# Scores by first and last 64 tokens instead of by even and odd tokens, in a fused gated-recurrence and bilinear FFN kernel

## The chip, the cores and the metric

The kernel runs on one core of one Trainium2 chip. The metric is the device time of one execution in microseconds (us); the number given for a kernel is the median of its runs. About 0.3% (0.6 us here) is what a measurement of this kernel can tell from no change.

## What is computed

A gated linear recurrence over 768 tokens, for 4 batches of 8 heads with head size 48, followed by a bilinear feed-forward network (FFN) over all 3072 tokens:

```
for t in range(S):                                   # S = 768, D = 48
    state = alpha[:, :, t, :, None] * state + einsum('bhd,bhe->bhde', k[:, :, t], v[:, :, t])
    y[:, :, t] = einsum('bhd,bhde->bhe', q[:, :, t], state)
x = y.transpose(0, 2, 1, 3).reshape(B * S, H * D)    # 3072 x 384
out = ((x @ w_a) * (x @ w_b)) @ w_out                # w_a, w_b 384 x 1536, w_out 1536 x 384
```

## The kernel before, in words

**Chunks.** The recurrence is computed in chunks. A chunk holds 256 tokens of two batches, and there are six (0 to 5). Each batch of a chunk is a "u" (0 or 1). A partition holds two neighbouring tokens, called r = 0 and r = 1 (even and odd); 128 partitions hold 256 tokens. The upper and the lower 64 partitions are two groups g of 128 tokens each. Within a group the attention is done directly, with a triangular mask; between groups a 48x48 state per head is carried.

**Order of the work.** `PROGRAM` is a list written out in full: each entry is a chunk number and operations, and the instructions of every engine are issued in exactly that order. There is no scheduler on the chip: a waiting instruction holds up all that stands behind it on its engine. The last letter of an operation names its engine: V VectorE (DVE in the profile), S ScalarE (ACT), P GpSimd (POOL), Y the queue of SyncE (SP).

**One chunk, operation by operation** (line numbers of the profile of before):

- `ld` (L549) loads alpha, k, q, v; `W` and `Wo` load the FFN's weights on GpSimd's queue.
- `ln`, `l2`/`l2s` (L564, L613), `H`/`L` or `R` (L623), `A2` or `AQ` (L633), `ra`, `E` (L667): logarithms of alpha, their sums of two tokens, the running sum on TensorE, the exponentials. `l2s` works on 64 partitions and moves them to the other 64.
- `lv` (L652) scales k and q of the r = 0 tokens, `mk` and `mq` (L678) write the scaled keys and queries into `QKp`.
- `C` + `Ce` (L736, L742, L744; chunks 0 and 1) or `T` (L767; chunks 2 to 5, a DMA transpose on SyncE's queue) transpose `QKp` into `kqT`.
- `v` (L785, L787) copies v from the loaded tile `v_t` into `vx`, whose heads stand 96 columns apart with zeros between.
- `K`/`K2` (L799, L812) and `k` (L826 to L830) update the state; `dk`, `de` or `dr`, `dl` supply its decay.
- `D` (L841) computes scores, `M` (L846) masks them on the way out of PSUM, or `Mc` (L850) copies them out and `Mm` (L854) masks the copy.
- `SB`, `SA` and `Y` (all through L865) sum y from the carried state and from the masked scores; `X` (L900, L902) copies y out of PSUM into `xT`.
- `a`, `b` (L919), `as` (L925), `pr` (L933), `o` (L941), `ot` (L956, L958), `st` (L974): the FFN. `a` and `b` each are 3 matmuls for one 128-wide block of the hidden layer; a `*` stands for all 512 tokens of the chunk, 0 or 1 for one half. `pr` multiplies the two, `o` is half of the output sum of 128 tokens (6 matmuls).

The FFN of chunk c is interleaved with the preparation of chunk c+1.

**Scores and inner sums before.** The keys of one parity rk (64 of them in a group) are the stationary operand, all 128 queries of the group the moving one, so that each matmul is 64x64 times 64x128. The four matmuls of the two groups g and of the two heads r of a pair sit in the four quadrants of the TensorE array and run side by side; four such matmuls are called a quad below. `D` is 4 quads, `Y` is 12. Tokens in y, `xT` and the scaled keys stand ordered by parity, and `pr` puts them back in order when it writes `prod`:

```
        o_, a_, b_ = tokens(ch.prod[:, f, :], us), columns(a[:, :n], n), columns(b, n)
        nc.vector.tensor_mul(o_, a_, b_)
```

Of the kernel before, what the change touches and what calls it, by code (L numbers as in the profile page):

```python
# [9 lines left out]
BF16 = mybir.dt.bfloat16  # L10
# [7 lines left out]
0: cm 0; c1; cz 0 b P; ci; ld a 0b Y; c1a; ld a 0a Y; ln 0b; cu; cz 1 b P; fill 7 2; cu2 V; cz 0 q V; cus; ld k 0b Y; ld k 0a Y; B 0b 5; ld q 0b Y; ld v 0 P  # L18
0: ln 0a; ld q 0a Y; E 0b b; E 0b i; mq 0b V; B 0a 0; E 0a i; dk 0 2; E 0a b; ld a 1 P; mk 0b V; C 0 1 5; cs 0 m P; ld k 1 P; ld q 1 P; v 0 S; mk 0a V; cm 1
0: de 0; fill 2 1; mq 0a V; C 0 0 3; Ce 0 1 V; W b 0 256; cz 0 v P; Ce 0 0 V; D 0 1 4; ln 1; ld v 1 P; W a 256 768; K 0 0 6; k 0 0 V; M 0 1; D 0 0 0; SB 0 6  # L20
0: cz 1 q P; B 1a 2; M 0 0; W a 0 256; E 1a i; E 1a b; W b 256 768; mq 1a V; mk 1a V; B 1b 4; dk 1 3; E 1b i; E 1b b; de 1; v 1 S; mq 1b V; mk 1b V; C 1 0 0
0: Y 0; SA 0; Ce 1 0 V; cs 1 m P
1: ld a 0 P; ld a 1 P
0: W a 768 1536; C 1 1 1; X 0 S; c2 P; D 1 0 3; W b 768 1536
1: ld q 0 P
0: Ce 1 1 V; K 1 0 5; k 1 0 V; a 4 0 0
1: ld k 0 P
0: D 1 1 6; SB 1 1
1: ld v 0 P; ld q 1 P
0: Mc 1 0; a 3 0 5; Wo 0 6; a 0 0 3; Mm 1 0 V; Mc 1 1; as 0 0; b 0 0 4  # L30
1: ld k 1 P
0: pr 0 0; b 1 0 6; a 2 0 3; a 1 0 7; a 5 0 4; as 2 0; b 2 0 3; Mm 1 1 V; as 1 0; b 4 0 7; as 5 0; b 5 0 4; pr 2 0; pr 1 0
1: ln 0
0: SA 1; Y 1; Wo 6 12; K 1 1 6; as 3 0; as 4 0; X 1 S
1: ra 0
0: K 0 1 3
1: l2 0 V
0: b 3 0 0; pr 5 0; pr 4 0
1: H 0 V; L 0 V
0: a 2 1 1; a 5 1 2; as 5 1; pr 3 0; a 1 1 7; b 4 1 5; b 5 1 4; as 2 1; k 0 1 V; pr 5 1; a 4 1 2; as 1 1  # L40
1: ln 1
0: b 2 1 0; pr 2 1; a 6 * 3; as 4 1; b 1 1 2
1: l2 1 V
0: pr 4 1; as 6 *
1: H 1 V
0: pr 1 1
1: A2 0 7
0: a 11 * 0; a 7 * 5; a 0 1 4
1: L 1 V
0: k 1 1 V  # L50
1: ra 1
0: as 11 *
1: lv 0 q V; E 0 i
0: as 0 1; b 6 * 0; b 11 * 3; a 8 * 4; pr 6 *; pr 11 *
2: ld a * P
0: b 0 1 1; as 8 *; a 3 1 6
1: E 0 b; lv 0 k V
0: a 10 * 2; pr 0 1
1: mq 0 V; ld v 1 P
0: b 8 * 4  # L60
1: A2 1 7
0: as 10 *; b 10 * 2; pr 8 *
1: E 1 b
0: as 3 1; as 7 *; b 9 * 3; b 3 1 0; b 7 * 1; a 9 * 6
2: ld q * P
1: v 0 S; lv 1 q V; mk 0 V
0: pr 10 *
1: mq 1 V; C 0 1 4
0: as 9 *
1: C 0 0 2  # L70
0: o 0 0 5; pr 7 *
1: dk * 6
2: ld k * P
3: ld v * P
0: cz 1 v P; pr 9 *
1: Ce 0 0 S; E 1 i; de *; lv 1 k P; Ce 0 1 V; D 0 1 1; D 0 0 3
0: pr 3 1
1: Mc 0 0; K2 0 0 7 0
0: o 1 0 6
1: mk 1 V; M 0 1  # L80
0: o 3 0 4; o 1 1 -; ot 1 S; c3 P
3: ld a * P
0: cs 1 0 P; o 3 1 -
1: k 0 0 V; k 0 1 V; Mm 0 0 V; SB 0 1; C 1 0 3; C 1 1 7
0: ot 3 S; o 0 1 -
1: Ce 1 0 V
2: ln *
1: v 1 V; D 1 0 3; Ce 1 1 S; K2 1 1 6 0; Y 0; SA 0
0: ot 0 V
1: k 1 0 V; D 1 1 6  # L90
0: o 2 0 5
1: M 1 0
2: l2 0 V
1: X 0 S; a 3 0 1; Mc 1 1
2: l2s 0 P; l2s 1 P
1: a 2 0 3; a 4 0 4
2: R 0
1: k 1 1 V; as 4 0
2: ra 1
1: as 3 0; b 4 0 7  # L100
0: o 2 1 -
1: as 2 0
0: ot 2 S
1: pr 4 0
2: R 1; lv 1 q P
1: b 3 0 6; b 2 0 7; a 5 0 2; pr 3 0; b 5 0 3; as 5 0; b 1 0 5; a 1 0 1; pr 5 0; pr 2 0; a 7 0 2; as 1 0; pr 1 0
2: AQ 3
1: SB 1 6
2: lv 0 k P
1: a 10 0 5  # L110
2: lv 1 k V; ra 0; ld v * P
1: Mm 1 1 V
2: E 1 b
1: as 10 0; b 10 0 0; pr 10 0
2: mq 1 V; E 1 i
1: as 7 0; b 7 0 1
2: E 0 b; E 0 i
1: a 0 0 5
0: st 3 Y
2: dr  # L120
1: SA 1; Y 1
2: mk 1 V
1: pr 7 0; a 11 0 0; a 6 0 3; b 6 0 2; X 1 S; b 11 0 4; a 2 1 6; as 6 0; a 3 1 7; as 11 0; b 2 1 1; pr 6 0
2: lv 0 q V
1: b 4 1 0; as 2 1
2: T 1
1: pr 11 0
2: dl
0: st 0 Y
1: a 0 1 2; pr 2 1  # L130
2: mq 0 V
1: b 3 1 3; b 0 0 6; as 3 1; as 0 0; b 0 1 7; pr 3 1; a 8 0 1; a 9 0 5
0: st 1 Y
1: b 8 0 3; b 9 0 4; pr 0 0; as 0 1
2: mk 0 V
1: a 4 1 2
3: ln *
1: a 9 1 6; pr 0 1; as 8 0; b 9 1 1
3: ra 1
1: b 10 1 7; pr 8 0; a 10 1 3; as 4 1; as 9 0; as 9 1; a 6 1 6; b 6 1 2; b 11 1 5; pr 4 1; as 10 1; pr 9 0; a 11 1 4; pr 10 1; pr 9 1; as 6 1  # L140
2: v 1 S
1: a 8 1 3; b 8 1 1; a 7 1 6; pr 6 1
3: l2 0 V
1: as 11 1
2: T 0
1: as 8 1; a 5 1 4
3: ra 0
1: as 5 1; a 1 1 2
2: v 0 V
4: ld a * Y  # L150
1: pr 11 1; as 7 1; pr 8 1
2: K2 * * 0 7; D 1 1 3; D 1 0 5
1: as 1 1; b 5 1 2; o 2 0 1
2: k * 0 V
1: pr 5 1
3: v 0 S; v 1 S
1: b 1 1 2
2: Mc 1 0; M 1 1
3: l2s 0 P; l2s 1 P
1: b 7 1 0; o 2 1 -; pr 1 1; o 3 0 4  # L160
2: SB 0 5
# [12 lines left out]
2: Mc 0 1
4: ln *
3: ld q * Y; ld k * Y
2: k * 1 V
3: AQ 2
2: Y 1; SA 1; Mm 0 1 V; Mm 0 0 V; Y 0; X 0 S
3: E 0 b  # L180
4: l2 0 V
2: X 1 V
1: o 0 1 -
2: b 1 * 6; a 1 * 5
3: E 1 b
4: ld k * Y
3: E 1 i
1: ot 0 S
3: E 0 i
4: l2s 0 P  # L190
2: a 0 * 0; b 0 * 1; as 0 *; as 1 *
3: lv 0 k P; lv 0 q P
2: a 5 * 7
1: st 3 Y
2: a 7 * 4
4: l2s 1 P
2: a 2 * 5
3: lv 1 q V; mq 1 V; lv 1 k V
2: pr 1 *
3: dr  # L200
2: pr 0 *
3: mk 0 V
4: ld q * Y
0: st 2 Y
2: as 5 *; a 6 * 6; b 6 * 2; as 7 *
3: mq 0 V
2: b 9 * 4; b 7 * 0
1: st 2 Y
3: dl
4: R 0  # L210
2: b 5 * 7
1: o 1 0 3
2: a 9 * 1; pr 7 *; as 6 *
3: T 0
2: pr 6 *
4: ra 0
2: pr 5 *; a 11 * 6
3: mk 1 V
2: as 9 *; a 3 * 0
4: lv 0 k V; lv 0 q V; R 1  # L220
2: as 2 *
1: o 1 1 -
2: as 11 *; a 8 * 5; b 11 * 2; a 4 * 7; b 2 * 1
3: T 1
1: ot 1 V
2: pr 9 *; as 8 *; pr 11 *; pr 2 *; b 8 * 3; b 4 * 5; as 4 *
5: ld a * Y
3: K2 * * 4 6
2: pr 8 *; as 3 *; pr 4 *
3: k * 0 V; D 0 0 2; Mc 0 0  # L230
2: b 3 * 1
4: ra 1
2: pr 3 *; b 10 * 5; a 10 * 0
# [171 lines left out]
def kernel(  # L405
# [14 lines left out]
    C = 128  # L420
# [678 lines left out]
```

## Time and profile before

| | |
|---|---|
| median of 3 runs | 193.84 us (193.75 to 194.29) |
| span of the profiled execution | 192.0 us (the page gives no other time of it) |
| TensorE busy | 186.8 us, 97% of the span |
| VectorE busy | 133.1 us, 69% |
| ScalarE busy | 106.5 us, 55% |
| GpSimd busy | 56.9 us, 30% |
| granted TensorE clock | 1.00 |

The median lies 1.8 us above the profiled span; what lies around the span is start and end of the execution. An engine's busy time is the union of its instructions. Matmuls are pipelined: one takes about 0.2 us from start to end while the next starts some ns later, so the pace of matmuls is read from how far a group of them reaches, not from the duration of one.

### The profile page before, as it was taken

Reading aid. Unit: us, or ns where it says so; the run is one execution under the profiler, and the core shown is the slowest. Engines: PE = TensorE matmul, PEld = TensorE weight load, DVE = VectorE, ACT = ScalarE, POOL = GpSimd, SP = SyncE. Lnnn points to the kernel's source line nnn. Section 1 sums busy time; section 2 is a strip of 40 time slices with the busy share of each in tenths; the row PEclk is TensorE's granted clock in tenths of the full one; section 3 lists DMA queues with packets and bytes.
Section 4 is the critical chain, followed back from the end, with each engine's and each line's share of the span. In section 5 each row is a group of like instructions: output and inputs, shape, how many; then the busy total and the mean of one; then the engine's idle time right before and its main releaser. Section 6 shows DMA issues by size and latency. Waiting matters only on the chain.

```text
span 192.0 us, 6086 instructions
## 1 busy us (share of the span) xinstructions
PE 186.8 (97%) x2613; PEld 116.9 (61%) x2613; DVE 133.1 (69%) x223; ACT 106.5 (55%) x194; POOL 56.9 (30%) x75
## 2 busy tenths in 40 slices
PE   7999999999999999999999999999999999999992
PEld 3888875677778876645557444656465644545562
DVE  2387698994989888899897956887567446252510
ACT  4448885656779867753487756743572435314211
POOL 8999626752450500640074262000000000000000
PEclk9999999999999999999999999999999999999999
DMA  5999999999969999999999989017641200000422
GB/s 132 274 219 218 251 253 235 244 269 264 251 107 166 165 216 265 248 254 149 233 213 181 156 174 129 3 42 140 146 66 44 85 0 0 0 0 3 164 82 82
DMA packets 62618, 29.40 MB, mean 153 GB/s; under 512 B 53712, under 2 KB 60768, under 8 KB 62592
## 3 DMA queue, kind: packets, MB, share of 16 engines
q0 software_dynamic: 18432, 13.37, 39.6%
q1 hardware_dynamic: 44016, 15.55, 38.1%
q8 instruction: 20, 0.33, 0.7%
q10 hardware_dynamic: 144, 0.10, 0.2%
q14 instruction: 6, 0.05, 0.1%
HBM read 25.98 MB, written 4.74 MB: 160 GB/s over the span
## 4 chain that ended last, share of the span: by engine, by line
PE 91%; DMA 5%; SPq 1%; DVE 1%; issue 1%; ACT 0%; DVEq 0%
PE psum L919 47%; PE psum L941 24%; PE psum L865 7%; PE psum L841 3%; DMA kqT<-QKp 3%; DMA q_t<-in_q_dram 3%; PE psum L736 2%; PE psum L633 1%; PE psum L952 1%; SPq L549 1%; PE psum L799 1%; PE psum L812 1%; PE psum L700 1%; PE psum L591 1%; PE psum L592 1%
## 5 line engine op out<-in xcount | busy, mean ns | idle before, releaser
L919 PE MATMUL psum<-xT,wb_t 128*128 128x512 bf16 (+1 forms) x270 | 56.0, 337 | 0.0
L919 PE MATMUL psum<-xT,wa_t 128*128 128x512 bf16 (+1 forms) x270 | 56.0, 337 | 0.0
L941 PE MATMUL psum<-wo_t,prod 128*128 128x384 bf16 x276 | 49.4, 326 | 0.0
L919 PEld LDWEIGHTS <-wb_t 128*128 128x128 bf16 x270 | 25.9, 98 | 19.9 <-issue 0.5
L919 PEld LDWEIGHTS <-wa_t 128*128 128x128 bf16 x270 | 25.9, 98 | 19.7 <-issue 0.3
L941 PEld LDWEIGHTS <-prod 128*128 128x128 bf16 x276 | 25.9, 98 | 17.6
L956 ACT ACTIVATE ot<-psum 128x384 f32<-128x384 f32 (+1 forms) x16 | 7.7, 482 | 22.7 <-PE psum L941 21.6
L850 ACT ACTIVATE m<-psum 128x1024 bf16<-128x1024 f32 x14 | 14.1, 1023 | 4.6 <-PE psum L841 4.3
L613 POOL TENSOR_TENSOR l<-la 64x384 f32<-64x384 f32 x7 | 7.8, 1108 | 26.6 <-ACT la L556 19.0
L846 DVE TENSOR_TENSOR m<-psum,mask 128x1024 bf16<-128x1024 f32 x10 | 12.1, 1220 | 3.1 <-PE psum L841 3.1
L652 POOL TENSOR_TENSOR q_t<-q_t,ra 128x384 f32<-128x384 f32 x5 | 6.1, 1215 | 22.5 <-ACT ra L645 19.7
L556 ACT ACTIVATE la<-a_t 128x1536 f32<-128x1536 f32 (+2 forms) x9 | 9.5, 1055 | 2.3 <-DMA a_t<-in_alpha_dram 2.2
L678 DVE TENSOR_TENSOR QKp<-q_t,beta 128x768 bf16<-128x768 f32 x10 | 10.0, 995 | 1.0 <-ACT beta L667 1.0
L865 PE MATMUL psum<-m,vx 64*64 64x128 bf16 x576 | 10.5, 217 | 0.0
L900 ACT ACTIVATE xT<-psum 128x768 bf16<-128x768 f32 x9 | 7.2, 816 | 5.7 <-PE psum L865 5.5
L678 DVE TENSOR_TENSOR QKp<-k_t,invb 128x768 bf16<-128x768 f32 x10 | 9.7, 972 | 0.8 <-ACT invb L667 0.8
L854 DVE TENSOR_TENSOR m<-m,mask 128x1024 bf16<-128x1024 bf16 x14 | 9.3, 684 | 1.2 <-ACT m L850 1.2
L958 DVE COPY ot<-psum 128x384 f32<-128x384 f32 (+1 forms) x9 | 4.8, 532 | 7.6 <-PE psum L941 4.7
L865 PEld LDWEIGHTS <-vx 64*64 64x64 bf16 x576 | 9.0, 107 | 0.5 <-issue 0.3
L841 PE MATMUL psum<-kqT 64*64 64x128 bf16 x384 | 9.0, 219 | 0.4 <-DMA kqT<-QKp 0.3
L652 POOL TENSOR_TENSOR k_t<-k_t,a_t 128x384 f32<-128x384 f32 x6 | 7.4, 1228 | 6.1 <-issue 3.3
L549 POOL DMA_DIRECT2D v_t<-in_v_dram x8 | 8.5, 1058 | 0.1
(271 smaller groups left out, 287.9 us busy)
## 6 DMA issues: line engine op xcount, KB each, us to landing
out_dram<-ot SPq DMA_DIRECT2D x23, 192.0 KB, 3.8
q_t<-in_q_dram SPq DMA_DIRECT2D x3, 768.0 KB, 6.5
a_t<-in_alpha_dram POOLq DMA_DIRECT2D x2, 768.0 KB, 15.2
k_t<-in_k_dram POOLq DMA_DIRECT2D x2, 768.0 KB, 12.1
v_t<-in_v_dram POOLq DMA_DIRECT2D x4, 384.0 KB, 7.0
a_t<-in_alpha_dram SPq DMA_DIRECT2D x2, 768.0 KB
k_t<-in_k_dram SPq DMA_DIRECT2D x2, 768.0 KB
a_t<-in_alpha_dram POOLq DMA_DIRECT2D x3, 384.0 KB, 8.5
```

The source lines that it names most:

```text
L549: eng.dma_start(out=t[:, us, hs].rearrange("p b h r d -> p (b h) (r d)"), in_=src[ch.b0 + us.start:ch.b0 + us.stop, hs, ch.s * 2 * C:(ch.s ...
L556: nc.scalar.activation(out=ch.la[:, us, hs].rearrange("p b h r d -> p (b h r d)"), in_=ch.a[:, us, hs].rearrange("p b h r d -> p (b h r d) ...
L613: eng.tensor_add(ch.l2[(1 - g) * HC:(2 - g) * HC, 1], x[:, :, 0, :], x[:, :, 1, :])
L652: eng.tensor_mul(x, x, by)
L678: eng.tensor_mul(QKp[ch.c % 2][:, u, j, :, hs, :D], src[:, u, hs].rearrange("p h r d -> p r h d"), f)
L841: nc.tensor.matmul(s2[g * HC:(g + 1) * HC, r, p, rk, :], lhsT=turned_part(ch, u, 1, rk, 2 * h + p, g, rs), rhs=queriesT(ch, u, 2 * h + p, ...
L846: nc.vector.tensor_mul(m.rearrange("p r a k s -> p (r a) (k s)"), ch.s2[u, h].rearrange("p r a k s -> p (r a) (k s)"), maskn(4))
L850: nc.scalar.activation(out=m.rearrange("p r a k s -> p (r a) (k s)"), in_=ch.s2[u, h].rearrange("p r a k s -> p (r a) (k s)"), func=AF.Copy)
L854: eng.tensor_mul(x, x, maskn(4))
L865: nc.tensor.matmul(y[c * DP:(c + 1) * DP, g, j // 2 * C:(j // 2 + 1) * C], lhsT=lhsT, rhs=rhs, start=(g, c) not in begun, stop=False, skip ...
L919: nc.tensor.matmul(p, lhsT=(wa_t, wb_t)[w][:, kk, f * 128:(f + 1) * 128], rhs=ch.xT[:, kk, us, :], start=(kk == 0), stop=(kk == KT - 1))
L941: nc.tensor.matmul(op, lhsT=ch.prod[:, f, at:at + C], rhs=wo_t[:, f, :], start=(f == 0), stop=(f == NFF - 1))
```

## The change

1. **Scores and inner sums.** Keys are taken by halves of a group: x = 0 is its first 64 tokens, x = 1 its last 64. Keys of x = 1 are seen only by queries of the last 64 tokens, so half of the matmuls in `D` and in `Y` have a moving operand of 64 columns instead of 128 (192 of 384 and 288 of 576). The number of instructions on TensorE stays the same.
2. **Masks.** Scores, mask and masked scores have 192 columns for a head pair and r instead of 256: `M`, `Mc` and `Mm` work on 128x768 instead of 128x1024.
3. **Keys.** The transposed keys must stand by halves. After `C` the transposes themselves write them so; after `T` a new operation `Tr` copies 128x1024 from `kqT` into a new tile `kp` (8 copies: 5 on VectorE, 3 on ScalarE).
4. **Values.** `v` still copies all of v; a new operation `vs` then copies, for one u and one g, two pieces of 32 partitions x 384 into the other 32 partitions (48 copies: 20 VectorE, 22 ScalarE, 6 GpSimd). `K` and `K2` now read v from `v_t`, not from `vx`.
5. **y.** `X` is done for each g apart (24 of 128x384: 11 VectorE, 13 ScalarE, where there were 12 of 128x768) and writes the tokens in order; `xT` is laid out by batch first. `pr` has no reordering any more.
6. **Placing.** The list is written anew. `l2s` is all on VectorE (8; before 1 there, 7 on GpSimd), `lv` is 16 on VectorE and 4 on GpSimd (before 9 and 11), `v` is 8 on VectorE and 4 on ScalarE (before 3 and 9). The loads of GpSimd's queue keep their order up to the last weights; the load of chunk 5's keys goes to SyncE's queue.

The core of the diff:

```diff
-            ch.kqT[u] = wk.tile([C, 2, 2, P2, C], BF16, name="kqT", bufs=4)
+            ch.kqT[u] = wk.tile([C, 16 * C], BF16, name="kqT", bufs=4)
...
+    def turn_keys(ch, u, eng):
+        t = alloc_t(ch, u)
+        x = wk.tile([C, 8 * C], BF16, name="kp", bufs=3)
+        ch.kp[u] = x.rearrange("p (h a q w) -> p h a q w", h=2, a=2, q=4)
+        ch.qT[u] = t[:, :8 * C].rearrange("p (r h a s) -> p h a r s", h=2, a=2, r=2)
+        evict(x.rearrange("p (y r s) -> p y r s", r=2, s=HQ), t[:, 8 * C:].rearrange("p (r y s) -> p y r s", r=2, s=HQ), eng)
...
+    def vswap(ch, us, g, eng):
+        for x in range(2):
+            to, of = (slice(g * HC + n * HQ, g * HC + (n + 1) * HQ) for n in (x, 1 - x))
+            o_ = vxs[ch.c % 2][to, us, 1 - x, :, :D]
+            i_ = ch.v[of, us, :, x, :]
...
+            evict(o_, i_, eng)
...
-            for rk in range(2):
+            for x in range(2):
                 for g in range(2):
                     for r in range(2):
                         rs = slice(r * DP, (r + 1) * DP)
-                        nc.tensor.matmul(s2[g * HC:(g + 1) * HC, r, p, rk, :], lhsT=turned_part(ch, u, 1, rk, 2 * h + p, g, rs),
-                                         rhs=queriesT(ch, u, 2 * h + p, g, rs), start=True, stop=True)
+                        nc.tensor.matmul(s2[g * HC:(g + 1) * HC, r, p, cols(x)], lhsT=keysT(ch, u, 2 * h + p, g, rs, x),
+                                         rhs=queriesT(ch, u, 2 * h + p, g, rs, x), start=True, stop=True)
...
-                        out_mm(ch, u, g, h, j, vx[gs, u, rk, at:at + DP], ch.m[u, h // 4][gs, h % 2, h // 2 % 2, rk, :])
+                        m = ch.m[u, h // 4][gs, h % 2 * 2 + h // 2 % 2, cols(x)].rearrange("p (r s) -> p r s", r=2)
+                        out_mm(ch, u, g, h, j, vx[gs, u, x, at:at + DP], m, x)
...
-            ch.xT = wk.tile([128, KT, B, C], BF16, name="xT")
...
+            ch.xT = wk.tile([128, B, KT, C], BF16, name="xT")
+        evict(ch.xT[:, 2 * u + g].rearrange("p a (s r) -> p a r s", r=2),
+              ch.y[u][0][:, g, :KT * C].rearrange("p (a r s) -> p a r s", a=KT, r=2), eng)
...
-        o_, a_, b_ = tokens(ch.prod[:, f, :], us), columns(a[:, :n], n), columns(b, n)
-        nc.vector.tensor_mul(o_, a_, b_)
+        nc.vector.tensor_mul(ch.prod[:, f, us.start * C:us.stop * C], a[:, :n], b)
```

The list, for the start of chunk 0 and for chunk 3's preparation beside chunk 2's FFN:

```diff
-0: ln 0a; ld q 0a Y; E 0b b; E 0b i; mq 0b V; B 0a 0; E 0a i; dk 0 2; E 0a b; ld a 1 P; mk 0b V; C 0 1 5; ...
+0: ld q 0b Y; B 0a 0; dk 0 4; E 0b i; mk 0b V; ld v 0 P; E 0b b; mq 0b V; C 0 1 5; ...
...
+2: Y 0; X 1 0 V
...
+1: o 1 0 0; o 1 1 -
...
+2: X 0 1 S; X 0 0 S; X 1 1 V; a 3 * 7; a 4 * 2; b 0 * 3; b 3 * 4; a 5 * 5; as 3 *; a 0 * 7
...
+3: T 0
+2: pr 9 *
+3: T 1
...
+5: ld q * Y; ld k * Y
...
+3: Tr 0 V
```

798 lines of the change are left out of this document (371 added, 427 removed).

## The prediction

> **What bounds the kernel now.** I read the page's busy times first, then its chain of work that ended last, then the windows by stage, then TensorE's timeline for the pace of the small matmuls, then the groups by form for what VectorE has to take over.
>
> ```profile
> span 192.0 us, 6086 instructions
> PE 186.8 (97%) x2613; PEld 116.9 (61%) x2613; DVE 133.1 (69%) x223; ACT 106.5 (55%) x194; POOL 56.9 (30%) x75
> PE 91%; DMA 5%; SPq 1%; DVE 1%; issue 1%; ACT 0%; DVEq 0%
> ```
>
> TensorE is busy for 97% of the span and is 91% of the chain. The windows cut at TensorE's own marks: the first FFN matmul (18.30) and the end of the last `Y` of chunks 1, 2, 3 and 4 (57.47, 78.06, 105.27, 130.88).
>
> ```profile
> core 0: us, PE busy (x) PEld busy (x) DVE busy (x) ACT busy (x) POOL busy (x), PEclk, DMA share, GB/s
> 57.47:78.06 20.59, 20.59 (x414) 16.22 (x415) 18.38 (x37) 15.59 (x29) 3.50 (x4) 1.00 1.18 204
> 78.06:105.27 27.21, 27.21 (x399) 14.71 (x400) 24.04 (x34) 16.89 (x29) 10.22 (x9) 1.00 1.07 212
> 105.27:130.88 25.61, 25.32 (x356) 13.43 (x356) 20.24 (x28) 15.15 (x27) 5.54 (x5) 1.00 0.65 98
> 57.47:130.88 73.41, 73.12 (x1166) 44.35 (x1167) 62.65 (x97) 47.62 (x84) 19.25 (x17) 1.00 0.95 170
> 18.30:188.69 170.39, 170.06 (x2342) 103.91 (x2336) 122.67 (x201) 96.33 (x175) 39.82 (x39) 1.00 0.76 148
> ```
>
> From 18.3 to the last matmul TensorE idles 0.3 us of 170, at full clock. So a column less on TensorE there is time, if nobody else becomes late; and the one that could is VectorE, at 62.65 of 73.41 us (85%) in the three middle stages, not at the 69% of the average.
>
> **TensorE's part.** Half of the quads of `D` and `Y` go from 128 to 64 columns. What a quad costs is its pace, read from how far a run of them reaches:
>
> ```profile
> 67.86 0.63 PE L841 MATMUL psum<-kqT 64*64 64x128 bf16 x32
> 94.61 0.69 PE L812 MATMUL psum<-vx,QKp 64*64 64x48 bf16 x64
> 129.01 0.87 PE L865 MATMUL psum<-m,vx 64*64 64x128 bf16 x48
> ```
>
> One matmul lasts 0.22 us (0.19 at 48 columns). So 32 with 128 columns step by (0.63 - 0.22)/31 = 13.2 ns, 48 by (0.87 - 0.22)/47 = 13.8 ns: 54 ns a quad. The 48-column ones of the state step by (0.69 - 0.19)/63 = 7.9 ns: 32 ns a quad. No row has 64 columns. In proportion to columns it would be 27 ns, the 48-column row says not below 32; I take 33, near that row because its weights have the same 64x64 form. That saves 21 ns a quad. Halved quads are 12 x 2 x 2 = 48 of `D` and 12 x 6 = 72 of `Y`; the 10 of chunk 0's first u lie before 18.3, where TensorE waits for others. 110 x 21 ns = **2.3 us**, between 0 and 110 x 27 ns = 3.0. Strided moving operands (two runs for queries) are in the 54 ns already, so `xT` by batch costs nothing; strided writes to PSUM (half of the `Y` matmuls, 32 transposes) no row shows: I take nothing for them, as for the strided reads, and if they ran at the pace of 128 columns the saving would go to the end 0.
>
> The Trainium skill, "TensorE: Matmul & The Clock Gate", sections "LDWEIGHTS (loading the stationary operand)" and "The mechanism", speaks against this: a weight load takes its columns divided by 1.2 in ns, and overlaps running matmuls only in another row group; for 64 columns that is an estimated 53 ns, and halving columns would bring nothing. The 48-column row, with the same weights at 32 ns a quad, does not agree. It is the second rival below.
>
> **The start.** The chain begins with the load of q.
>
> ```profile
> 7.81 0.56 DVE L678 TENSOR_TENSOR QKp<-q_t,prod 128x384 bf16<-128x384 f32 x1 [3.63 <-DMA q_t<-in_q_dram]
> 8.29 1.06 DVE L678 TENSOR_TENSOR QKp<-k_t,prod 128x384 bf16<-128x384 f32 x2
> 8.94 0.62 PE L736 MATMUL psum<-ident,QKp 128*128 128x128 bf16 x8 [0.15 <-DVE QKp L678]
> ```
>
> Before, `mq 0b` waits for q and `mk 0b` comes behind it, although k is loaded ahead of q. Now `mk 0b` comes first, so the transposes can start after `mq 0b`, at about 8.4 instead of 8.94. Further on, `B 1b` no longer stands behind `M`'s waits, `K` needs no copied v, and y is evicted by two engines (0.55 each beside the other, instead of 0.82). Following the new list with these rows, the first FFN matmul comes at about 18.6 with everything of chunk 0's second u ahead of it issued, which before is reached at about 19.2. I take **-0.5 us**, from 0 to -1.0: the first weights land near 18.5 (issue at 12.08, 6.4 us to landing) in the unchanged order of GpSimd's queue.
>
> **VectorE's part.** Rows used, with those that the change replaces:
>
> ```profile
> L846 DVE TENSOR_TENSOR m<-psum,mask 128x1024 bf16<-128x1024 f32 x10 | 12.1, 1220 | 3.1 <-PE psum L841 3.1
> L613 POOL TENSOR_TENSOR l<-la 64x384 f32<-64x384 f32 x7 | 7.8, 1108 | 26.6 <-ACT la L556 19.0 <-issue 5.8 <-PE psum L633 1.7
> L854 DVE TENSOR_TENSOR m<-m,mask 128x1024 bf16<-128x1024 bf16 x14 | 9.3, 684 | 1.2 <-ACT m L850 1.2
> L902 DVE CAST xT<-psum 128x768 bf16<-128x768 f32 x3 | 2.9, 952 | 2.4 <-PE psum L865 2.4
> L744 DVE COPY kqT<-psum 128x1024 bf16<-128x1024 bf16 x6 | 4.1, 688 | 2.5 <-PE psum L736 2.4
> L787 DVE COPY vx<-v_t 128x768 bf16<-128x768 bf16 x3 | 1.1, 350 | 0.0
> ```
>
> It takes over 7 `l2s` and 7 `lv` (0.55 each on VectorE, 1.1 to 1.2 on GpSimd): +7.7. Five more `v` at 0.35: +1.8. Twenty copies of `vs`, which no row shows: half of the 128x768 copy would be 0.2, a 384-wide row in f32 is 0.55; I take 0.2 since it is the same copy in bf16: +4.0 (up to 11). Five `kp` copies, between 0.35 and the 0.69 from PSUM, taken as 0.35 x 1024/768 = 0.47: +2.4. `X`: 11 x 0.55 - 3 x 0.95 = +3.2; three more `ot` +1.7; two `Ce` fewer -1.4. The masks lose a quarter of their elements: 10 x 0.27 + 14 x 0.15 = -4.8. Five VectorE instructions beside a GpSimd one took 0.2 to 0.8 longer than their like (for instance `lv` 1.35 at 80.58), in sum 2.4, most of which goes with GpSimd's work. In all about +12: 145 of 190 us.
>
> In the three middle stages the new list adds 7 `lv`, 5 `l2s`, 3 `mk`/`mq`, 4 `v`, 12 `vs` copies, 3 `kp`, and 5 half `pr` (0.44), 16 us by these rows with masks and `X`; neighbouring rows overlap by some 0.08 us each (-3.4 for 43 instructions), less 2.3 for GpSimd: 62.7 + 10.3 = **73 us**. TensorE's list in the same stretch is 73.4 + 5.2 (7 more half blocks, 2 `o`, sums) - 60 x 0.021 = 77.3. VectorE fits, at 94%, with little to spare. ScalarE goes from 48 to about 55 there (22 `vs` copies in all at half of `v`'s 0.85): it fits.
>
> **New waits.** After each `T` a copy `Tr` stands ahead of `D`. Chunk 2's second `T` is covered by some 9 half blocks and 4 other entries, about 6.3 us against 5.1 for the transfer and 0.5 to 1.0 for the copy; what is queued behind a late `Tr` on VectorE are the `pr`, and behind those TensorE for PSUM banks. `X` behind chunk 2's `Y` is covered by two `o` (1.95 us) against 1.3 on ScalarE. The `v` loads now also wait for `K` and `vs` to have read the tile; behind them on GpSimd's queue stand `lv`s and loads that are needed several us later. Chunk 5's k on SyncE's queue stands behind chunk 3's two `T` and its q, and waits for `mk` of chunk 3, which `T` needs anyway; chunk 4's `T` comes long after. So nothing for the move. Following VectorE's list through chunk 2's FFN, I find it at most about 1 us behind TensorE and the banks free in time. I take **+0.8 us** for all these together, 0 to 3.7.
>
> Sum on the profiled execution: 192.0 - 2.3 - 0.5 + 0.8 = 190.0 of span; the 1.8 us by which the median lies above the span stays, as the last output sum, its eviction and its store keep their form. **191.8 us.**
>
> **Rivals.** *VectorE becomes the bound* (slower). Place: the three middle stages. For it: 94% of demand, in order, each late `pr` keeps a bank. If a `vs` copy takes 0.55 and a `kp` 0.69, 73 becomes 73 + 12 x 0.35 + 3 x 0.22 = 78, and if GpSimd's remaining copies and loads still hold VectorE up for 2.3 us, 80 to 81: 3.7 more than TensorE's 77.3, hence 195.5. It decides from about 77, 4 us above my sum. Against: rows for plain bf16 copies are short, and at 80 to 92 us VectorE already was at 97% with TensorE never idle. *Weight loads set the pace*: no gain on TensorE, 193.84 - 0.5 + 0.8 = 194.1, or 193.3 without new waits. For: 32 ns for 48 columns is more than columns cost in proportion. Against: it is still far below 54. *The copies behind `T` are exposed*: TensorE waited 0.29 us for a `T` in chunk 3 already. Four chunks with 0.5 to 1.0 each (1.02 for 128x1024 on ScalarE) are 2 to 4 us in place of my 0.8: 193 to 195. *The change does less than it says* is the second rival.
>
> **Chances.** My forecast 0.58; VectorE bound 0.20; weight loads 0.10; copies behind `T` 0.12. About 0.6 us either way can't be told from no change. Faster by more: 0.58 and 0.04 of the last two = 0.62. Within: 0.11, from the same two. Slower: 0.20 + 0.07 = 0.27. The likeliest case alone spans 190.1 (3.0 saved, 1.0 at the start, some waiting) to 193.0. The range reaches up to VectorE's 195.5, less its tail, and leaves 2 in 10 out: 190.0 to 195.2.
>
> **What would show it.** Right: `D` with 32 matmuls reaching some 0.08 us less far, and 48 of `Y` 0.13 less; TensorE idle below 1.5 us after 18; VectorE near 145 busy and above 90% from chunk 1's last `Y` to chunk 4's; `vs` copies near 0.2. Wrong: `D` and `Y` groups as long as before; or TensorE idle several us before `a`, `b` with `pr` as the releaser; or before `D` with `kp`.

## The result, and the profile after

The changed kernel takes **196.14 us** (median of 4 runs, 195.88 to 196.83) against 193.8 for the kernel before (193.52 to 194.29) on the same chip: a ratio of **1.0113, 95% interval 1.0091 to 1.0134**. It is slower, by 2.3 us between the medians and 2.2 by the ratio; 191.8 was forecast. Executions that lay 1.5% or more above the fastest of their kernel (in e3, e4, e7, e12, e14 and e19) are left out of every ratio, and differences in time below are taken from the ratios. The page of the profiled execution (span, busy times, chain that ended last):

```profile
span 194.4 us, 6135 instructions
PE 185.8 (96%) x2612; PEld 115.6 (59%) x2613; DVE 146.3 (75%) x276; ACT 113.9 (59%) x217; POOL 44.0 (23%) x66
PE 37%; DVE 5%; issue 2%; ACT 0%
```

TensorE's busy time fell by 1.0 us while the span grew by 2.4. The chain is now followed for only 44% of the span, and VectorE is 5% of it. The windows, cut at the last `Y` of chunks 1 to 4 (54.10, 78.50, 106.90, 135.85):

```profile
core 0: us, PE busy (x) PEld busy (x) DVE busy (x) ACT busy (x) POOL busy (x), PEclk, DMA share, GB/s
54.10:78.50 24.40, 24.17 (x452) 18.82 (x444) 23.91 (x56) 20.77 (x44) 0.59 (x2) 1.00 1.02 179
78.50:106.90 28.40, 26.61 (x404) 13.94 (x393) 24.93 (x45) 17.02 (x31) 2.14 (x2) 1.00 1.12 210
106.90:135.85 28.95, 27.25 (x385) 14.55 (x380) 28.33 (x43) 17.46 (x32) 8.08 (x9) 1.00 0.67 106
54.10:135.85 81.75, 78.03 (x1222) 47.31 (x1216) 77.17 (x141) 55.24 (x105) 10.80 (x13) 1.00 0.93 164
```

Before, TensorE idled 0.3 us in the three middle stages; now 81.75 - 78.03 = 3.7 us, in the second and third of them. VectorE is at 94% over the three and at 98% in the last (28.33 of 28.95). TensorE's timeline shows both halves of the story:

```profile
86.42 0.81 PE L886 MATMUL psum<-xT,wb_t 128*128 128x512 bf16 x3 [0.59 <-DVE prod L899]
...
98.88 0.54 PE L812 MATMUL psum<-kqT,kp 64*64 64x128 bf16 x32 [0.75 <-DVE kp L924]
...
105.69 1.27 PE L841 MATMUL psum<-m,vx 64*64 64x128 bf16 x96
...
120.09 0.81 PE L886 MATMUL psum<-xT,wa_t 128*128 128x512 bf16 x3 [1.47 <-DVE prod L899]
```

32 matmuls of `D` reach 0.54 us (0.63 before), and 96 of `Y` reach 1.27: the small matmuls did get faster. The brackets are the new idle time: matmuls of `a` and `b` wait for `pr` (a product frees a PSUM bank), and `D` waits for the copy `kp`.

To add this up I took the start times of all matmuls from the trace and summed, from 17 us on, what every gap has over the usual step (216 ns for 512 columns, 163 for 384, 109 for 256, 60 for the small ones), where that is more than 0.11 us. That gives 0.59 us before and 6.18 after, 5.6 more. Without these gaps `D` and `Y` together take 15.76 us before and 13.56 after; the other kinds of matmul lose 0.6 more. So 187.2 us from first to last matmul become 187.2 - 2.2 - 0.6 + 5.6 = 190.0. The change saved what it was to save on TensorE and lost more than twice of it in waits.

The waits lie in three places: 1.4 us before 80 us, spread out; 0.75 at 85 and 2.18 at 113 to 120, for products; 1.82 between 97 and 105, which begin with a transfer. VectorE's timeline around that last place, and ScalarE's:

```profile
95.84 0.68 DVE L899 TENSOR_TENSOR prod<-as__2050,psum 128x512 bf16<-128x512 bf16 x1
98.39 0.43 DVE L924 COPY kp<-kqT 128x1024 bf16<-128x1024 bf16 x1 [1.87 <-DMA kqT<-QKp]
```

```profile
101.84 1.48 ACT L529 ACTIVATE la<-a_t 128x1536 f32<-128x1536 f32 x1 [1.03 <-DMA a_t<-in_alpha_dram]
```

`Tr` of chunk 3 stands 1.87 us for the transposing DMA `T`, and behind `T` on SyncE's queue the alpha of chunk 5 is late for its logarithm. Why `T` is late shows on GpSimd, whose queue loads v. After:

```profile
87.68 0.99 POOL L625 TENSOR_TENSOR q_t<-q_t,ra 128x384 f32<-128x384 f32 x1 [32.99 <-DMA q_t<-in_q_dram]
88.63 1.19 POOL L522 DMA_DIRECT2D v_t<-in_v_dram  x1
```

and before:

```profile
97.16 1.00 POOL L652 TENSOR_TENSOR q_t<-q_t,ra 128x384 f32<-128x384 f32 x1 [13.30 <-ACT ra L645]
98.11 1.32 POOL L652 TENSOR_TENSOR k_t<-k_t,a_t 128x384 f32<-128x384 f32 x1
99.37 1.20 POOL L549 DMA_DIRECT2D v_t<-in_v_dram  x1
```

The load of chunk 4's v is issued 10.7 us sooner, as the steps that held GpSimd's queue before it now run on VectorE. In the trace's DMA records the transposes are packets of 256 bytes and v's loads packets of 192. Before, chunk 3's `T` (two transposes of 2048 packets each) runs from 86.8 to 93.1 us (6.3) with no load of v beside it; after, from 88.5 to 97.9 (9.4), and all 2048 packets of chunk 4's v lie inside, from 91.4 to 97.4. The first transpose, which ends before v begins, takes 2.8 us there, the second 5.3, from 92.6.

### The profile page after: what moved, and what is told of

Its sections match the earlier page's. It is cut to its first block, busy times and chain, and to the rows that moved or that the text cites. A ratio compares the mean times of both kernels' runs of the same rounds, so it can differ in the third digit from the quotient of the medians.

```text
span 194.4 us, 6135 instructions
## 1 busy us (share of the span) xinstructions
PE 185.8 (96%) x2612; PEld 115.6 (59%) x2613; DVE 146.3 (75%) x276; ACT 113.9 (59%) x217; POOL 44.0 (23%) x66
## 5 line engine op out<-in xcount | busy, mean ns | idle before, releaser
L825 ACT ACTIVATE m<-psum 128x768 bf16<-128x768 f32 x14 | 11.1, 808 | 5.2 <-PE psum L812 5.2
L924 DVE COPY ot<-psum 128x384 f32<-128x384 f32 (+1 forms) x12 | 6.4, 540 | 10.0 <-PE psum L907 10.0
L924 POOL COPY vx<-v_t 32x384 bf16<-32x384 bf16 x6 | 4.8, 801 | 37.5 <-PE psum L886 21.8
L922 ACT ACTIVATE vx<-v_t 32x384 bf16<-32x384 bf16 x22 | 11.4, 520 | 2.9 <-DVE vx L746 2.5
L821 DVE TENSOR_TENSOR m<-psum,mask 128x768 bf16<-128x768 f32 x10 | 9.5, 954 | 4.0 <-ACT ot L922 3.2
L841 PE MATMUL psum<-m,vx 64*64 64x64 bf16 (+1 forms) x576 | 9.1, 205 | 0.1
L922 ACT ACTIVATE xT<-psum 128x384 bf16<-128x384 f32 x13 | 7.4, 601 | 2.5 <-PE psum L841 2.1
L625 POOL TENSOR_TENSOR q_t<-q_t,ra 128x384 f32<-128x384 f32 x1 | 1.0, 990 | 33.0 <-DMA q_t<-in_q_dram 33.0
L829 DVE TENSOR_TENSOR m<-m,mask 128x768 bf16<-128x768 bf16 x14 | 7.5, 553 | 1.0 <-ACT m L825 0.9
L924 DVE CAST xT<-psum 128x384 bf16<-128x384 f32 x11 | 6.2, 585 | 2.1 <-PE psum L841 1.8
```

What stands on the lines that cost most here:

```text
L821: nc.vector.tensor_mul(m, x, maskn())
L825: nc.scalar.activation(out=m, in_=x, func=AF.Copy)
L829: eng.tensor_mul(m, m, maskn())
L841: nc.tensor.matmul(o, lhsT=lhsT, rhs=rhs, start=(g, c) not in begun, stop=False, skip_group_check=True)
L922: nc.scalar.activation(out=o_, in_=i_, func=AF.Copy)
L924: eng.tensor_copy(o_, i_)
```

## The experiments

Ratios are against the kernel before, run beside each of the five sets; its medians there were 194.0 to 194.4.

**e1. The columns alone.** The kernel before, with the `D` and `Y` matmuls of the odd keys cut to 64 columns, nothing else moved (and the first warm-up matmuls spread over PSUM banks). Tokens stand by parity here, so this leaves out scores that the reference needs.

```diff
-  s2[..., rk, :], rhs=queriesT(...)
+  s2[..., rk, rk * HC:], rhs=qT[:, 1:2] if rk else qT
```

> The kernel of before with one edit: the matmuls of the odd keys in D and Y have 64 columns instead of 128 (so y is not the reference's); list, copies, masks and placing stay as they were, the seven filling matmuls at the start go to different banks. If a 64-column quad costs 33 ns, 110 quads after the first FFN matmul save 21 ns each: 2.3 us, so about 191.5 (ratio 0.988), with Y's 48 matmuls reaching some 0.13 us less far. If the weight loads set the pace: 193.8 and groups as long as before.

192.13 us, ratio 0.9896 (0.9871 to 0.9922): -2.0 us. `Y`:

```profile
102.35 0.69 PE L867 MATMUL psum<-m,vx 64*64 64x128 bf16 x48
```

0.69 for 48 matmuls against 0.87 before. The saving is real, and weight loads don't eat it. By the sum above, `D` and `Y` take 12.8 us here, 2.9 less than before; 0.5 us of gaps came new.

**e6. The change in the old order.** The changed functions run by the list of before, with `vs` right behind each `v`, `Tr` right ahead of the first `D`, and `X` in halves.

```diff
-0: v 0 S
+0: v 0 S; vs 0 0 S; vs 0 1 V          (so at each v; X u -> X u 0 S; X u 1 V; Tr u V ahead of the first D)
```

> The whole change in the list of before: lv and l2s stay where they were, chunk 5's k on GpSimd's queue; each v is followed by its two vs (ScalarE, VectorE), Tr on VectorE stands just ahead of the first D of its u, X is one half on ScalarE and one on VectorE. If the new placing, with 14 more lv and l2s on VectorE, is what costs: faster than the changed kernel, 192 to 194, since VectorE gets only some 6 us of vs, 3 of kp and 3 of X and loses 4.8 on masks. If the change's own copies cost the time whatever the placing: 195 to 197.

214.13 us, ratio 1.1063 (1.1017 to 1.1109), gaps 19.2 us. The list of before with these copies is worse by far, 20 us over the kernel before. So for this change the new list as a whole is the better one; what in it is still late is the question.

**e2 and e3. Fewer copies on VectorE and GpSimd.** e2 is the changed kernel without `vs`, so that half of the inner products read values left from another chunk; e3 gives GpSimd's six `vs` copies to ScalarE.

```diff
-3: vs 1 0 V; vs 0 0 V          (e2: all 24 entries)
-4: vs 1 0 P
+4: vs 1 0 S                    (e3: the three entries with P)
```

> The changed kernel without any vs (values of two quarters stay in the wrong place, so the output is not the reference's). It takes 20 copies of 0.25 us from VectorE, 22 of 0.52 from ScalarE and 6 of 0.8 from GpSimd. If VectorE's load and what holds it up in the middle stages makes TensorE wait (5.5 us more waiting than before), 5 us less on VectorE of which 3 lie in the middle, and no GpSimd copies beside it, should give back 2 to 4 us: 192 to 194. If the copies behind T or the order of the list are the cause: no more than 0.5 us, 195.6.

> The changed kernel with GpSimd's three pairs of vs (chunks 4 and 5) on ScalarE. If GpSimd's copies holding up VectorE at 112 to 119 us (mq 1.76 instead of 0.95, l2s 1.26 instead of 0.55, vs 0.5 instead of 0.25, about 2.3 us in sum) cause the 2.2 us that TensorE waits from 113 to 120: 194 to 194.5. If it is VectorE's load or order alone: 196.

e2: 196.89 us, ratio 1.014 (1.0116 to 1.0165); e3: 199.94, ratio 1.0295 (1.0267 to 1.0323). Less work, and no gain. e2 on GpSimd, ScalarE and TensorE:

```profile
90.33 2.34 POOL L513 DMA_DIRECT2D v_t<-in_v_dram  x2
```

```profile
105.64 1.48 ACT L520 ACTIVATE la<-a_t 128x1536 f32<-128x1536 f32 x1 [6.08 <-DMA a_t<-in_alpha_dram]
```

```profile
108.57 3.58 PE L898 MATMUL psum<-wo_t,prod 128*128 128x384 bf16 x12 [2.88 <-ACT ot L913]
```

The gaps at 85 and 113 to 120 us (2.9 us) are gone, as VectorE's load would have it. But two loads are issued at 90.33, not one: GpSimd's `vs` steps had stood between the loads of chunk 4's and chunk 5's v, and without them both go out. 4096 packets of v run from 93.7 to 105.2 us beside chunk 5's alpha, which lands 6.08 us late for ScalarE; behind it stands `ot`, and TensorE waits 2.88 us. In e3, where the same steps leave GpSimd, the two loads run from 92.1 to 104.7, and `T` takes from 89.3 to 99.6.

**e7, e8, e9, e4. Four tries on the queue and on `Tr`.** The logarithm's late alpha first pointed to the order on SyncE's queue.

```diff
 (e7; e8 is e7 without vs)
-5: ld a * Y        behind 3: T 1
+5: ld a * Y        ahead of 3: T 0
 (e9)
-5: ld q * Y; ld k * Y
+5: ld q * Y        and  5: ld k * Y  behind  1: st 0 Y
 (e4)  all Tr left out, D reads kqT with the keys in the wrong order
```

> The changed kernel with one issue moved: chunk 5's alpha is loaded on SyncE's queue ahead of chunk 3's two transposing DMAs instead of behind them. Theory A (the loads of chunk 5 come late on SyncE's queue, ScalarE's logarithm of chunk 5 waits for alpha, and what is queued behind it on ScalarE holds up TensorE): the 1.03 us wait of that logarithm disappears, and the time goes from 196.1 to about 195.0 us; more, if the transposes are also less crowded by alpha (the copy of the turned keys waited 1.87 us for them). Theory B (VectorE's added work bounds the middle stages): at most 0.3 us better, since VectorE's 98% in the fourth stage stays.

> As the run before, with the 48 copies of v in exchanged order left out (the output is not the reference's: half of the inner products read rows that nobody wrote in this chunk). Without the copies alone the time was 196.9 us, with a wait of 6.08 us for chunk 5's alpha on ScalarE and 3.01 us of TensorE idle behind it. Theory A: that wait goes, and the time is 191 to 193 us, as halved columns alone gave 192.1. Theory B, too, expects 191 to 193 once the wait is gone, as VectorE has lost about 7 us of copies; what the two differ in is how much of it is seen against the run with the copies and the early alpha: A expects under 1 us between the two, B over 2 us.

> The changed kernel with chunk 5's keys issued on SyncE's queue one store later (behind the store of the second chunk's first tile instead of right behind chunk 5's queries). Theory A with contention (three loads of 768 KB on one queue share the bandwidth, so alpha lands later because queries and keys run beside it): alpha lands earlier than 7.4 us after its issue, the wait of 1.03 us goes, time about 195.0. If the keys do not crowd alpha (they are issued 4.2 us after it): no change, 196.1 within 0.4. Theory B: no change.

> The changed kernel without the eight copies that reorder the turned keys: the score matmuls read the turned tile as it lands (the output is not the reference's: the keys are in the wrong order). Theory B': the copies are on the path between the transposing DMA and the scores (kp waited 1.87 us for the DMA and took 0.43, scores then waited 0.75 for kp), so 0.4 us at each of up to eight tiles and 3.8 us of VectorE's load go: 194.5 to 195.2 us. Theory A: about 0.5 us better (195.6), as the scores wait for the transposing DMA all the same. If the copies cost nothing: 196.1.

Ratios: e7 1.0159 (1.0115 to 1.0202), e8 1.0292 (1.0254 to 1.0329), e9 1.0145 (1.0118 to 1.0172), e4 1.0105 (1.0077 to 1.0133). None helps. With alpha ahead, the transposes come later (in e8 from 90.2 to 102.0 us, with two loads of v inside; its second transpose is issued 5.5 us behind the first) and `D` waits in place of the logarithm. The keys' place on the queue is worth nothing that can be seen, and without `Tr` the scores wait for `T` itself. In e4 and e9 the gap of 1.64 us that ends near 120 stays as it was. So these changes of the order on SyncE's queue do not cure it, and the copy behind `T` is not what costs while `T` itself is late (its price with `T` on time no run shows); what runs beside `T` came next.

**e10, e11, e12, e13. When chunk 4's v is loaded.** e10 holds the load until `T` has landed, by a copy of one element on GpSimd; e11 is e10 without `vs`; e12 is e10 with two products put ahead of six steps for later chunks on VectorE; e13 is the kernel before with this load sooner.

```diff
 (e10, e11, e12)
+3: gatet 1
 4: ld v * P
 (e13, on the kernel before)
+4: ld v * P; lv 1 q P
-4: lv 1 q P
 4: lv 1 k P
-4: ld v * P
```

> The changed kernel with one thing added: ahead of the load of chunk 4's v GpSimd copies one element of the second turned tile of chunk 3, so that the load cannot start before the two transposing DMAs have landed. Theory C (with pairs and levels moved to VectorE, GpSimd is idle and issues that load at 88.6 us instead of 99.4, and its 192-byte packets share the DMA engines with the transposes from 90 to 97 us; the transposes take 9.6 us instead of 7, VectorE stands 1.87 us for them, and alpha of chunk 5, next on the same queue, lands late): the transposes end some 2.5 us sooner, the copy's wait of 1.87 us and the logarithm's of 1.03 go, and of TensorE's waits between 97 and 105 us (0.91, 0.18, 0.37, 0.36) at least 1 us; the time is about 194.7, down to 193.5 if VectorE's backlog in the next stage shrinks too. Theory B (VectorE's load alone): at most 0.5 us better, 195.6 or more.

> As the run before, without the 48 copies of v in exchanged order (half of the inner products then read rows that nobody wrote in this chunk). Without the copies alone the time was 196.9, with 0.75 and 2.18 us of TensorE's waits gone at 85 and at 113 to 118 us and 3 us come new behind chunk 5's late alpha. Theory C: with the load out of the transposes' way that wait is gone, and the time is 191.0 to 192.5, that is the copies cost 2 to 3.5 us where the loads do not hide it. If C is wrong the alpha is late again and the time stays over 195.

> As the first run of this set, with the products of two feed-forward tiles of chunk 3 put ahead of six steps of VectorE for chunks 4 and 5 (a cast and a copy of v, the pairs of l and their crossed forms, the low parts). They are the products for which TensorE waited 0.39, 0.15 and 1.64 us between 113 and 119 us. If those waits come from the order on VectorE alone, 1.5 to 2 us less than the first run, about 193; if VectorE has no room there at all, the waits come back at the next product or at chunk 4's transposes, and the time is that of the first run within 0.5.

> The kernel before with only the load of chunk 4's v moved ahead on GpSimd's queue, in front of the two level steps that hold it until 99.4 us. Theory C: the load runs beside chunk 3's transposes, which take about 2.5 us longer; the scores of chunk 3 and chunk 5's logarithm come later, and the time grows by 0.5 to 2 us (194.7 to 196.2). Theory B expects no change (194.2 within 0.4).

e10: 202.13 us, ratio 1.0417 (1.0382 to 1.0452); e11 1.0269 (1.023 to 1.0309), e12 1.0429 (1.0387 to 1.0472), e13 193.94, 1.0005 (0.9976 to 1.0034). Half of the theory held: in e10 `T` takes 5.1 us (89.5 to 94.6), the gaps at `D` and the logarithm's wait are gone. The price is new: v now starts at 100.8, beside chunk 5's q and k, lands at 106.7, and the new list has put the copy of that v on VectorE ahead of chunk 3's masks:

```profile
107.11 0.36 DVE L740 COPY vx<-v_t 128x768 bf16<-128x768 bf16 x1 [4.40 <-DMA v_t<-in_v_dram]
```

TensorE stands 4.2 us behind it, and behind that its granted clock is 0.5 for 3.4 us. In e11 both loads of v run from 100.6 to 111.4, and TensorE stands 5.4 us. In e12 the waits for the two products (2.2 us in e10, from 118 to 125) are gone, but 1.6 us come back at 128 and the time is no better: the move by itself brought nothing. Later is wrong; and e13 shows that sooner is free: there v's packets ran from 86.0 to 90.7, all but 223 of them ahead of the transposes. So e13 put almost nothing beside `T`, and it does not test the 0.5 to 2 us that were expected of the two running together.

**e14, e15, e16. The load ahead of `T`.** The load is put in front of the `lv` that waits for chunk 4's q, behind a one-element copy of chunk 4's k. e15 is e14 without `vs`, e16 is e14 with three steps of chunk 5 given to GpSimd.

```diff
 (e14, e15, e16)
-4: l2s 0 V; ra 1; lv 1 q P
+4: l2s 0 V; ra 1; gate k 0; ld v * P; lv 1 q P
 ...
-4: ld v * P
 (e16)  5: l2s 0, l2s 1, lv 0 q   V -> P
```

> The changed kernel with the load of chunk 4's v moved ahead on GpSimd's queue: not behind the level step that waits for chunk 4's queries, but behind a copy of one element of chunk 4's keys (landed at about 81 us), so that its packets run at 82 to 88 us, before chunk 3's transposes. Theory C (the shared transfers are part of the loss): VectorE's wait of 1.87 us for the transposes and the logarithm's wait of 1.03 us go, TensorE's waits between 97 and 105 us fall from 1.8 to under 1.0, time 194.5 to 195.5. Theory B (VectorE's load alone): no change, 196.1 within 0.4; the waits of 0.75 and 2.2 us at 85 and 113 to 118 stay under both.

> As the run before, without the 48 copies of v in exchanged order (half of the inner products then read rows that nobody wrote in this chunk). If the transfers and the copies are the whole of the loss: 191 to 192.5, as halved columns alone gave 192.1. If the time stays above 194, a third cause is left, and it is another wait for a transfer that the trace will name.

> As the first run of this set, with three steps of chunk 5 that the change has on VectorE between 111 and 118 us given to GpSimd (the two crossed pairs of l, 0.55 and 1.26 us, and one level of q, 0.55 us). Theory B: TensorE's 2.2 us of waits for products at 113 to 118 us fall to under 1, the time to 1 to 1.5 us below the first run. If GpSimd's instructions hold up VectorE's beside them instead (a product with beta took 1.76 us there instead of 0.95), the waits stay and the time is that of the first run within 0.4.

e14: 195.03 us, ratio 1.005 (1.0022 to 1.0078), 1.2 us of the loss back, and the interval lies below that of the changed kernel. e16: 194.45, ratio 1.0025 (1.0003 to 1.0048), 0.5 us more, which is within what can be told. In e16 `kp` waits for nothing any more:

```profile
96.33 0.42 DVE L917 COPY kp<-kqT 128x1024 bf16<-128x1024 bf16 x1
98.08 0.42 DVE L917 COPY kp<-kqT 128x1024 bf16<-128x1024 bf16 x1
```

its gaps from 95 to 107 us are 0 (1.82 after), those from 107 to 130 fall from 2.18 to 0.87. Most of this came with the load alone: in e14's trace (of an execution of 197.5 us) they are 0 and 1.02. What came new in both is a gap of 1.3 to 1.5 us near 90 (0.75 after, at 85). e15, again, is no price of the copies: 197.01, ratio 1.017 (1.0139 to 1.02); without GpSimd's copies its queue went on to chunk 5's v, which ran from 93.2 to 99.3, `T` took from 90.0 to 99.9, and `D` waited 2.54 us.

**e17, e18, e19. The price of the copies, and two more repairs**, all on e14. e17 leaves out the copies of VectorE and ScalarE and keeps GpSimd's, so that its queue keeps its pace (part of the inner products then read values left from another chunk). e18 gives all 14 pairs and levels back to GpSimd. e19 is e16 with four copies moved into a gap of VectorE:

```diff
-3: lv 1 k V; vs 1 0 V; vs 0 0 V
+3: vs 1 0 V; vs 0 0 V; lv 1 k V          (e19)
-2: l2s 0 V
+2: l2s 0 P          (e18; so the 14 entries of l2s and lv that had P)
```

> Chunk 4's v loaded ahead of the transposes, and the exchanged copies of VectorE and ScalarE left out while GpSimd's, which pace its queue, stay (part of the inner products then read rows that nobody wrote in this chunk). If the earlier runs without copies were slow only because GpSimd's queue issued chunk 5's v early: no wait for a transpose over 1 us, and 192 to 193.5 us, so that the copies on VectorE and ScalarE are worth 1.5 to 3 us of the 195.0. If the time stays at 195 or more, the copies cost nothing and something else holds the kernel.

> Chunk 4's v loaded ahead of the transposes, and all 14 pairs and levels that the change moved from GpSimd to VectorE given back. Theory B: VectorE loses some 8 us, TensorE's waits for products at 85 and 113 to 118 us go, time 193.5 to 194.2. If GpSimd's instructions hold up VectorE's, or its queue then issues chunk 4's or 5's v at a bad time: 195 or more.

> Chunk 4's v ahead of the transposes, three steps of chunk 5 on GpSimd, and four exchanged copies of chunk 3 (1.04 us in sum) put ahead of the level step that waits 0.88 us for chunk 3's keys, so that VectorE does them in that gap. If order on VectorE is what makes the products late at 86 us: TensorE's wait of 1.32 us there falls to 0.3 to 0.6, time 193.3 to 193.9 (194.45 without the move). If not: 194.45 within 0.4.

e17: 192.78 us, ratio 0.9926 (0.9905 to 0.9948). This is the price of the 42 copies, 20 of them on VectorE, with the loads in place: 1.005 - 0.9926 is 1.24% of 194, 2.4 us. Chunk 3's `T` takes 5.1 us there (90.5 to 95.6), as in e10. And e17 is only 0.3% (0.6 us) above e1: of the 4.2 us between e1 and the changed kernel, 1.2 are the load's place and 2.4 the copies. e19: 194.18, ratio 1.0001 (0.9985 to 1.0017); the gap of 1.32 us that ends at 88 us in e16 is 0.37. e18: 200.12, ratio 1.0318 (1.0286 to 1.0351), by a place that no expectation names:

```profile
50.59 0.82 PE L834 MATMUL psum<-m,vx 64*64 64x128 bf16 x48 [2.94 <-POOL vx L479]
```

Chunk 2's pairs, back on GpSimd, stand ahead of a fill of `vx` with zeros that chunk 1's `Y` needs; behind this wait, too, the granted clock is 0.5 for 3.4 us. So e18 does not tell what the 14 steps cost on VectorE.

The three repairs of e19 bring the new layout level with the kernel before, not below it. No version that leaves nothing out was faster than the kernel before.

## Why the prediction was wrong

**TensorE's saving: right.** Taken were 33 ns for a quad of 64 columns and 2.3 us in all. A matmul with 64 columns, which ends these groups of `Y` now, lasts 0.19 us. So the 96 of `Y` step by (1.27 - 0.19)/95 = 11.4 ns where they stepped by 13.8, and a halved quad takes 4 x (2 x 11.4 - 13.8) = 36 ns; the 48 of e1 step by (0.69 - 0.19)/47 = 10.6, which gives 30. Without gaps `D` and `Y` lose 2.2 us, and e1 brings 2.0 in time. The rival of the weight loads fell with e1. (e1 has no strided writes, and its sum falls by 2.9; which part of the 0.7 between them is the strided writes, for which nothing was taken, no run took apart.)

**The start: forecast too large, and a small term.** The first FFN matmul came at 18.9, not 18.6; with the 19.2 to which it was compared that is 0.3 in place of 0.5, and a new gap of 0.36 that ends at 22.3 us takes it.

**VectorE's sum: right over the whole, 4 us short in the middle, and its reading wrong.** 145 us were forecast for the whole, 146.3 came. In the middle stages 73 were forecast and 77.2 came. That the share, 94%, is the one forecast is luck: TensorE's stretch grew as well, from 77.3 forecast to 81.75, for the most part by its waits. The rows alone sum up to 16.4 us more than before, where 16 were taken; the 2.3 that were to go with GpSimd's steps did not go, and rows overlap by 1.8 us more, not 3.4. By form:

```profile
L924 DVE COPY vx<-v_t 32x384 bf16<-32x384 bf16 x20 | 5.8, 292 | 0.3
L586 DVE TENSOR_TENSOR l<-la 64x384 f32<-64x384 f32 x8 | 5.1, 641 | 0.5 <-ACT la L529 0.3
L924 POOL COPY vx<-v_t 32x384 bf16<-32x384 bf16 x6 | 4.8, 801 | 37.5 <-PE psum L886 21.8 <-DVE vx L746 15.4
L924 DVE COPY kp<-kqT 128x1024 bf16<-128x1024 bf16 x5 | 2.1, 423 | 1.9 <-DMA kqT<-QKp 1.9
```

A `vs` copy took 0.29 (0.2 taken), a `kp` 0.42 (0.47). The step that failed here is "VectorE fits, at 94%, with little to spare". A sum over three stages says nothing on the order inside one. In the third, VectorE did this:

```profile
109.32 0.95 DVE L651 TENSOR_TENSOR QKp<-q_t,beta 128x768 bf16<-128x768 f32 x1
...
111.06 0.35 DVE L746 COPY vx<-v_t 128x768 bf16<-128x768 bf16 x1
111.44 0.55 DVE L586 TENSOR_TENSOR l<-la 64x384 f32<-64x384 f32 x1
112.00 1.00 DVE L924 COPY vx<-v_t 32x384 bf16<-32x384 bf16 x2
113.03 0.69 DVE L899 TENSOR_TENSOR prod<-as__2391,psum 128x512 bf16<-128x512 bf16 x1
113.64 0.55 DVE L625 TENSOR_TENSOR q_t<-q_t,ra 128x384 f32<-128x384 f32 x1
114.11 1.76 DVE L651 TENSOR_TENSOR QKp<-q_t,beta 128x768 bf16<-128x768 f32 x1
115.79 0.68 DVE L899 TENSOR_TENSOR prod<-as__2412,psum 128x512 bf16<-128x512 bf16 x1
116.39 0.79 DVE L537 TENSOR_TENSOR l<-la 128x384 f32<-128x384 f32 x1
117.19 1.26 DVE L586 TENSOR_TENSOR l<-la 64x384 f32<-64x384 f32 x1
118.48 0.96 DVE L596 TENSOR_TENSOR lh<-l 128x768 f32<-128x768 f32 x1
119.36 0.68 DVE L899 TENSOR_TENSOR prod<-as__2432,psum 128x512 bf16<-128x512 bf16 x1
```

There is no idle time, and three products in 9 us, with steps for chunks 4 and 5 ahead of each; TensorE waits for each (0.39, 0.15 and 1.64 us). GpSimd's steps still hold VectorE up: the product with `beta` took 1.76 at 114.11, where its like took 0.95 at 109.32, and the pairs 1.26 at 117.19, where they took 0.55 at 111.44, both beside GpSimd's remaining copies and levels. In this trace the 15 steps of that shape (`mk` and `mq`) with nothing of GpSimd beside them took at most 0.96. The first rival had a part of the mechanism (late products), and its 195.5 was nearest to what came; its point of decision, 77 us of VectorE work, was reached (77.2). The transfers that met, the other part, no rival had.

**New waits: the term that failed.** Taken were +0.8 us (0 to 3.7); the gaps grew by 5.6. Part by part (the copies and the order were each measured on top of e14 and can stand for the same waits, so their prices are not to be added):

- *Loads on GpSimd's queue.* The text asked only what comes later on that queue ("the `v` loads now also wait"). What came was sooner: with 14 steps gone from it, the queue reached the load of chunk 4's v 10.7 us earlier and put it beside `T`. e14 prices it at 1.2 us. The cover that the text worked out, 6.3 us against "5.1 for the transfer", was for chunk 2's second `T` alone; chunk 3's, the late one, had none. (The 0.29 us that TensorE waited for a `T` before is chunk 4's, at 111.50, not one of chunk 3.)
- *Copies.* The 2.4 us of e17 are the second part, where the text had room for the copies of VectorE and ScalarE at no price.
- *Order on VectorE.* e16 and e19 got back 0.5 us each by moving three steps and four copies. Each alone is within what can be told; together, from 1.005 to 1.0001, they are clear of it.
- *Chunk 5's keys on SyncE's queue: "nothing"* held, as far as e9 can say: later was no better.

The copies behind `T`, the third rival, were not what was exposed: `Tr` of chunk 3 stands 1.87 us for `T`, and without the copies (e4) the time was the same.

What stays open: 1.4 us of gaps before 80 us, which no run took apart; how the copies' 2.4 us divide between VectorE and ScalarE; and what the 14 steps taken over from GpSimd cost on VectorE.

## What to carry to other kernels

An in-order queue that mixes arithmetic with loads is also a clock for the loads. Take the arithmetic away and the loads behind it go out sooner, into whatever transfer then runs: for every step that leaves such a queue, look up the next load behind it, its new issue time, and what it will run beside. And here an engine at 94% over three stages was at 98% in one of them: compare the instructions between two products with the time that TensorE's free banks give, stage by stage, before saying that it fits.

An experiment that leaves work out can move a load as well. e2, e11 and e15 looked as if the copies were free; only e17, which kept the copies that pace the queue, gave them a price.

## What the hardware showed that was not expected

**Two queues on the same DMA engines.** Chunk 3's transposes (4096 packets of 256 bytes) took 5.1 to 6.3 us with no packet of v beside them or almost none (e10, e17, e2, before) and 9.4 to 12 us with v's packets of 192 bytes from GpSimd's queue beside them (after, e15, e3, e8). In e8 and e15 a part of that is a late issue of the second transpose (5.5 and 4.4 us behind the first). The second by itself tells more: its 2048 packets took 5.3 to 6.5 us beside v in these four runs, and the first, with at most 1.5 us of v's packets beside it, 2.8 to 3.5. The DMA records of 90 to 99 us, first after, then e16; columns are packets, MB and share of the engines' time:

```profile
q1 hardware_dynamic: 3798, 1.20, 74.2%
q0 software_dynamic: 2064, 0.39, 52.4%
```

```profile
q1 hardware_dynamic: 6456, 1.77, 106.0%
q0 software_dynamic: 501, 0.09, 12.3%
```

With 1563 packets more on GpSimd's queue, SyncE's moved 2658 fewer in the same 9 us. The Trainium skill, "DMA: Bandwidth & Descriptors", section "Queues, rings and completion order", says that each DMA engine takes turns between the queues with work, a packet at a time. The trace agrees so far: while v's packets run, both queues move, and the second transpose takes about twice as long as the first (5.3 us for 2.8 in the changed kernel). What its packet is in the trace's records, which are single pieces of 256 or 192 bytes, no run shows.

**The clock after a wait.** In e2 TensorE waited 2.88 us, and its output sums then ran at half the clock (the twelve took 3.58 us; twelve took 2.12 in the changed kernel):

```profile
107.00:108.00 1.00, 0.00 (x0) 0.00 (x0) 0.26 (x1) 0.91 (x3) 0.00 (x0) 1.00 1.21 269
108.00:109.00 1.00, 0.43 (x2) 0.26 (x2) 0.00 (x0) 1.00 (x4) 0.00 (x0) 0.59 1.23 273
109.00:110.00 1.00, 1.00 (x5) 0.46 (x3) 0.00 (x0) 1.00 (x4) 0.00 (x0) 0.50 1.24 282
110.00:111.00 1.00, 1.00 (x5) 0.46 (x3) 0.86 (x1) 0.98 (x3) 0.00 (x0) 0.50 0.39 123
111.00:112.00 1.00, 1.00 (x6) 0.50 (x5) 1.00 (x3) 0.00 (x0) 0.00 (x0) 0.70 0.09 26
```

The granted clock (the third column from the end) is 0.5 from about 108.2 to 111.6 us, 3.4 us. So this wait of 2.9 us cost some 1.5 us more. e15 fell to 0.5 as well, behind a wait of 2.54. In the traces of this case every wait of 2.5 to 5.4 us (e2, e7, e8, e10, e11, e12, e15, e18) has such a fall, and single waits of up to 1.8 us (e3, e8) have none; in e6 it fell behind shorter waits that stood close together. The Trainium skill, "TensorE: Matmul & The Clock Gate", section "What's actually happening", gives about 3.4 us without work as what drops the clock and as long of work to bring it back; the second agrees with the trace, the first was shorter here.
